# A decode attention kernel: the last group's output sum moves from two halves of 288 columns to four quarters of 144, stored as 8 rows

## Chip, cores and metric

The kernel runs on one core of one Trainium2 chip. The metric is the device time of one execution in microseconds (us). The core has five engines with a queue each: TensorE (PE; its weight loads are listed apart as PEld), VectorE (DVE), ScalarE (ACT), GpSimd (POOL) and SyncE (SP), which here only issues DMA transfers. Matmuls write into PSUM, where a bank holds 512 float32 columns in each of 128 partitions; everything else lies in SBUF.

## What is computed

Two independent problems, A and B, each one decode step of attention over the last 4096 positions of a key and value cache, with 2 batch rows, 32 query heads that share 16 key/value heads in pairs, and 128 elements a head. The two outputs of 576 columns are put side by side.

```python
def _A_ref(x, k_cache, v_cache, wq, wo):          # _B_ref is the same
    B, Sq, D = x.shape                            # 2, 1, 576
    Hq, Dh = 32, 128
    Hkv, Sk = k_cache.shape[1], k_cache.shape[2]  # 16, 16384
    W = min(4096, max(256, Sk // 4))
    rep = Hq // Hkv
    q = (x @ wq).reshape(B, Sq, Hq, Dh).transpose(0, 2, 1, 3)
    k = jnp.repeat(k_cache[:, :, Sk - W:, :], rep, axis=1)
    v = jnp.repeat(v_cache[:, :, Sk - W:, :], rep, axis=1)
    scores = jnp.einsum("bhqd,bhkd->bhqk", q, k) * (Dh ** -0.5)
    p = _softmax(scores, axis=-1)
    o = jnp.einsum("bhqk,bhkd->bhqd", p, v)
    return o.transpose(0, 2, 1, 3).reshape(B, Sq, Hq * Dh) @ wo
...
return jnp.concatenate([a, b], axis=-1)
```

Everything is bfloat16 in memory. Reading the caches, wq and wo moves 153 MB.

## The kernel before

The program is written out by hand: `S.add` appends an operation to one engine's queue with a list of the operations that it depends on, and the loops from line 834 to line 923 fix the order on every queue. Waits on semaphores are derived from the dependencies when the queues are emitted (line 976). A DMA is an operation of SP (`dma_op`) with a semaphore of its own kind.

**Stages.** The two problems' 16 key/value heads are handled in 16 steps `s` (8 for A, 8 for B), each of which covers 4 pairs of batch row and key/value head. A step loads a 4 MB slab of K and one of V into a ring of four (`issue_slab`, line 239). DVE transposes the K slab in four pieces (`do_X`, L515), PE multiplies with the queries into the PSUM tile `ST[s % 2]` (`do_S`, L540 and, through the helper `matmul_again`, L188), ACT takes the exponential (L585), DVE transposes the result, and PE multiplies with V into `ACC` (`do_PV`, L631). That last product uses four column groups of the array: `ACC[32*cb:32*cb+32]`, cb from 0 to 3, all in one bank.

**Groups.** Two steps make a group G (0 to 7; 0 to 3 are problem A). A group's attention outputs are normalised (`do_norm`) into `oTg`, spread over a mask (`om`), redistributed on PE (`do_redist`, L739) and copied by ACT into `Rsb` (L757): one column per batch row and head slot, so that a head's two batch rows are a weight matrix of 128 x 2. `do_proj` (line 766) multiplies with that head's 128 rows of wo. For groups 0 to 6 (`by_group`) the 576 output columns go to `OT` (512, L786) and to a bank of the pair `TB` (the other 64, through L188), and the 64 columns are summed in `o_rest` (L802, L805).

**The last group.** For group 7 the wo rows come last of all, in four DMAs: `wo3` (line 291) for its first step, and `issue_last` (line 277), three transfers `wl0` (heads 0 and 1), `wl1` (head 2), `wl2` (head 3) for its second. Ahead of them, once group 6 is done, the sum so far is moved into the PSUM tile `ST[0]`, which is free by then. `fin(half)` names where (line 763): half 0 is partitions 0 and 1 of the first bank, half 1 partitions 32 and 33 of the second bank, 288 columns each. The move is `fin0` on ACT (L810), `fin1` on DVE (L811, the 64 columns of `o_rest` and `TB`) and `fin2` on DVE (L813, 224 columns). All three are in the list `fin_ops`, of which the last is waited for by three idle matmuls on PE (line 749) and by the first step's projection. The projection of the last group is line 790: each of 4 + 4 heads is two matmuls of 288 columns, in two column groups. The weights of the first four heads are `Rsb[1][:, :, s]`, of the last four `oTn[:, h, :]`, which `do_norm` writes directly (L719).

**The end.** `do_E(1)` casts the two halves to bfloat16 into `out_sb[1]`, which is the tile `pR`: ACT takes half 0 (L822), DVE half 1 (L823). `do_out` (line 830) stores 2 rows of 576 elements, 1152 bytes each, with one DMA; SP waits for it at the end (line 985). Problem A's output is stored by the same function from `out_A`, whose issue stands just ahead of it in SP's queue. The other masks are slices of the tile `masks` (lines 156 and 157).

Of the kernel before, what the change touches and what calls it, by code (L numbers as in the profile page):

```python
# [5 lines left out]
FP32 = mybir.dt.float32  # L6
# [53 lines left out]
def build_kernel(nc, probs, out, cfg=None):  # L60
# [30 lines left out]
    NOUT = wo0.shape[1]  # L91
    NH = NOUT // 2
    NB0 = 512
    NB1 = NOUT - NB0
    assert NOUT % 2 == 0 and 0 < NB1 <= NB0
    SCALE = float(Dh) ** -0.5
# [10 lines left out]
    def by_group(G):  # L107
        return G < NG - 1
# [5 lines left out]
    with es:  # L114
# [36 lines left out]
        maskB = sb("maskB", [128, 512], BF16)  # L151
        oTn = sb("oTn", [128, 4, Bb], BF16)
        oTg = [sb("oTg%d" % n_, [128, n], BF16) for n_, n in enumerate((64, 32))]
        om = sb("om", [128, 2, 256], BF16)
        Rsb = [sb("Rsb%d" % n_, [128, Bb, n], BF16) for n_, n in enumerate((32, 16))]
        masks = sb("masks", [128, 30], BF16)
        maskS, mask16D, maskA, mask4S, maskJ, maskP = (masks[:, a_:b_] for a_, b_ in ((0, 8), (8, 16), (16, 20), (20, 24), (24, 28), (28, 30)))
        mask16S = sb("mask16S", [128, 16], BF16)
# [5 lines left out]
        acc_r = sb("acc_r", [128, 2, 128], BF16)  # L164
        o_rest = sb("o_rest", [Bb, NB1], FP32)
        ident_r = sb("ident_r", [128, 32], BF16)
        out_A = sb("out_A", [Bb, NOUT], BF16)
        out_sb = [out_A[:, :], pR[0:Bb, 0:NOUT]]
        ps = lambda name, shape: es.enter_context(nc.psum_tensor(name, shape, FP32))
# [514 lines left out]
        def do_norm(D_):  # L684
# [5 lines left out]
            if by_group(G):  # L690
# [23 lines left out]
                return  # L714
            dst = oTn[:, :, :].rearrange("d (t r) b -> d b t r", t=2) if sl else \
                oTg[u % 2][:, 0:8].rearrange("d (b r t) -> d b t r", b=Bb, r=2)
# [14 lines left out]
        def do_redist(u, idle=0):  # L731
# [22 lines left out]
            if u >= 2:  # L754
                g2, n2 = UNITS[u - 2]
                deps.append(proj[2 * (g2 + n2 - 1) + 1])
            r_ev[u] = S.add("act", lambda e: e.activation(  # L757
                Rsb[u % 2][:, :, 0:NS], bank[:, 0:NS * Bb].rearrange("d (b s) -> d b s", b=Bb), ACTF.Copy), deps, "rev%d" % u)
            tb_consumer[n] = r_ev[u]

        fin_ops = []

        def fin(half):
            return ST[(ND - 2) % 2][32 * half:32 * half + Bb, 512 * half:512 * half + NH]

        def do_proj(D_):
# [4 lines left out]
            w0 = wo_slot(G)  # L771
            new = G % GPP == 0
            if by_group(G):
                parts = [([(Rsb[u % 2][:, :, s0 + s_], s_) for s_ in range(8)], [r_ev[u], wo_dma[G]], new, True, True)]
            elif D_ < ND - 1:
                parts = [([(Rsb[u % 2][:, :, s_], s_) for s_ in range(4)], [r_ev[u], wo_dma[G]] + fin_ops, False, False, False)]
            else:
                parts = [([(oTn[:, h, :], 4 + h) for h in hs], [norm[D_], wo_last[n_]], False, False, n_ == len(HEADS) - 1)
                         for n_, hs in enumerate(HEADS)]
            for lhs, deps, start, rstart, rstop in parts:  # L780
                def f(e, rest, lhs=lhs, start=start, rstart=rstart, rstop=rstop):
                    last = None
                    for n_, (l_, s_) in enumerate(lhs):
                        begin, end = n_ == 0, n_ == len(lhs) - 1
                        if by_group(G):
                            first = e.matmul(OT[0:Bb, 0:NB0], l_, wob[:, w0 + s_, 0:NB0], start=start and begin, stop=end, skip_group_check=True)  # L786
                            last = matmul_again(e, first, rest[0:Bb, 0:NB1], wob[:, w0 + s_, NB0:NOUT], rstart and begin, rstop and end)
                        else:
                            for half in range(2):
                                last = e.matmul(fin(half), l_, wob[:, w0 + s_, half * NH:(half + 1) * NH],  # L790
                                                start=False, stop=end, skip_group_check=True)
                    return last
                deps = deps + [e_ops[(P - 1, 0)]]
                if by_group(G):
                    n, bank, proj[D_] = tb_job(f, "proj%d" % D_, deps)
                    rest_at[G] = bank
                    if G % GPP < GPP - 1 and G < NG - 2:
                        d = [proj[D_]]
                        if new:
                            if P:  # L800
                                d.append(e_ops[(P - 1, 1)])
                            rest_add[G] = S.add("dve", lambda e: e.tensor_copy(o_rest[:, :], bank[0:Bb, 0:NB1]), d, "rest%d" % G)  # L802
                        else:
                            d.append(rest_add[G - 1])
                            rest_add[G] = S.add("dve", lambda e: e.tensor_tensor(o_rest[:, :], o_rest[:, :], bank[0:Bb, 0:NB1], ALU.add),  # L805
                                                d, "rest%d" % G)
                        tb_consumer[n] = rest_add[G]
                    elif G == NG - 2:
                        d = [proj[D_], chain[(ND - 2, "exp")], chain[(ND - 2, "max")]]
                        a_ = S.add("act", lambda e: e.activation(fin(0), OT[0:Bb, 0:NH], ACTF.Copy), d, "fin0")  # L810
                        tb_consumer[n] = S.add("dve", lambda e: e.tensor_tensor(  # L811
                            fin(1)[:, NB0 - NH:NH], o_rest[:, :], bank[0:Bb, 0:NB1], ALU.add), d + [rest_add[G - 1]], "fin1")
                        fin_ops.append(S.add("dve", lambda e: e.tensor_copy(fin(1)[:, 0:NB0 - NH], OT[0:Bb, NH:NB0]), [a_], "fin2"))  # L813
                    else:
                        rest_at[G] = (n, bank)
# [3 lines left out]
        def do_E(P):  # L819
            G = (P + 1) * GPP - 1  # L820
            if G == NG - 1:
                e_ops[(P, 0)] = S.add("act", lambda e: e.activation(out_sb[P][:, 0:NH], fin(0), ACTF.Copy), [proj[2 * G + 1]], "Elo%d" % P)  # L822
                e_ops[(P, 1)] = S.add("dve", lambda e: e.tensor_copy(out_sb[P][:, NH:NOUT], fin(1)), [proj[2 * G + 1]], "Ehi%d" % P)  # L823
                return
            n, bank = rest_at[G]
            e_ops[(P, 1)] = tb_consumer[n] = S.add("dve", lambda e: e.tensor_tensor(
                out_sb[P][:, NB0:NOUT], o_rest[:, :], bank[0:Bb, 0:NB1], ALU.add), [proj[2 * G + 1], rest_add[G - 1]], "Ehi%d" % P)
            e_ops[(P, 0)] = S.add("act", lambda e: e.activation(out_sb[P][:, 0:NB0], OT[0:Bb, 0:NB0], ACTF.Copy), [proj[2 * G + 1]], "Elo%d" % P)

        def do_out(P, c0, c1, eng, deps):  # L830
            dma_op(eng, out_sem, 1, lambda e: e.dma_start(
                out[:, 0, P * NOUT + c0:P * NOUT + c1], out_sb[P][:, c0:c1]).then_inc(out_sem, 16), deps, "out%d_%d" % (P, c0))

# [88 lines left out]
        for P in range(NPROB):  # L922
            do_out(P, 0, NOUT, "sp", [e_ops[(P, 1)], e_ops[(P, 0)]])

# [99 lines left out]
```

## Time and profile before

| | |
|---|---|
| median of 3 runs | 362.61 us (362.55 to 362.83) |
| the execution with the profile | 363.02 us |
| its span, first to last instruction | 361.8 us |
| mean granted TensorE clock | 0.882 of full speed |
| loads | 153.10 MB, 423 GB/s over the span |
| DVE transposes of K, L515 | 145.3 us busy in 64 instructions |
| matmuls with the queries, L540 and L188 | 111.6 and 110.1 us |
| cast of half 0, L822, ACT, 2x288 | 400 ns |
| cast of half 1, L823, DVE, 2x288 | 449 ns |
| move of the sum: L810, L811, L813 | 361, 222, 393 ns |
| issue of the last store, L831 | 263 ns |

The profile gives each engine's busy time, the span in 40 equal slices (digits are tenths), the waits between engines and the chain that ended last, which is followed back from the last instruction through whatever released each step. In a line of the timeline stand start and length in us, engine, line of the code, operation, what is written and read, and the shape; "128*2" is the part of the PE array that is used, "x4" a count, and the bracket the idle time before it with what ended it. "SPq" is SP's queue of DMA issues. Times of instructions are of the profiled execution.

### The profile page before, as it was taken

How to read it: one execution, taken by the hardware profiler on the slowest of the kernel's cores; microseconds unless marked ns; L12 is line 12 of the kernel's file. 1: busy time of each engine (PE TensorE's matmuls, PEld its weight loads, DVE VectorE, ACT ScalarE, POOL GpSimd, SP SyncE). 2: the span in 40 equal slices, each digit the busy share in tenths (PEclk: the TensorE clock that was granted, in tenths of full speed). 3: DMA queues.
4: the chain of work that ended last, by engine and by line, in shares of the span. 5: the costliest groups of instructions: out<-in, count | busy, mean ns of one | idle time of the engine just before them, and what ended most of it. 6: DMA issues, size and time to landing. Idle time of an engine off the chain costs nothing.

```text
span 361.8 us, 2730 instructions
## 1 busy us (share of the span) xinstructions
PE 218.6 (60%) x1318; PEld 55.8 (15%) x945; DVE 200.9 (56%) x175; ACT 68.2 (19%) x149; POOL 35.3 (10%) x55
## 2 busy tenths in 40 slices
PE   0399195763747207466574737766867707657786
PEld 0010021120111101112120201212121201211132
DVE  4112599846647019283756658392919239079931
ACT  1036502130203002103020203020201203002131
POOL 1000000004000400001300040002100040200020
PEclk9999689997889857969698978899898978969999
DMA  8999999999999999999999999999999999999996
GB/s 348 421 449 406 464 406 437 431 408 453 415 442 438 428 424 438 429 428 438 417 446 422 435 428 442 426 435 428 424 424 440 431 424 433 431 438 428 438 409 248
DMA packets 6491, 153.27 MB, mean 424 GB/s; under 512 B 712, under 2 KB 1232, under 8 KB 1616
## 3 DMA queue, kind: packets, MB, share of 16 engines
q1 hardware_dynamic: 6476, 153.10, 98.8%
q8 instruction: 9, 0.15, 0.2%
q14 instruction: 2, 0.02, 0.0%
q10 hardware_dynamic: 4, 0.00, 0.0%
HBM read 153.10 MB, written 0.00 MB: 423 GB/s over the span
## 4 chain that ended last, share of the span: by engine, by line
DMA 72%; DVE 17%; PE 7%; ACT 3%; SPq 1%; issue 0%
DMA ring<-in_B_k_cache_dram 34%; DMA ring<-in_A_k_cache_dram 27%; DVE xt L515 14%; DMA wob<-in_B_wo_dram 8%; DMA wob<-in_B_x_dram 3%; PE st L188 3%; PE st L540 3%; ACT wob L465 1%; DVE wob L475 1%; ACT qk L483 1%; PE st L450 1%; DVE m L550 1%; ACT wob L470 1%; DVE nM L563 0%; SPq L252 0%
## 5 line engine op out<-in xcount | busy, mean ns | idle before, releaser
L515 DVE STREAM_TRANSPOSE xt<-ring 128x2048 f32<-128x2048 f32 x64 | 145.3, 2284 | 86.6 <-DMA ring<-in_A_k_cache_dram 49.8
L540 PE MATMUL st<-xt,zq 128*128 128x512 bf16 x256 | 111.6, 436 | 122.6 <-DVE xt L515 98.1
L188 PE MATMUL st<-xt,zq 128*128 128x512 bf16 x256 | 110.1, 430 | 0.0
L540 PEld LDWEIGHTS st<-xt,zq 128*128 128x128 bf16 x256 | 27.1, 106 | 216.3 <-DVE xt L515 113.5
L631 PE MATMUL acc<-ring,pC 128*32 128x512 bf16 x512 | 32.5, 381 | 1.2 <-DMA ring<-in_B_v_cache_dram 1.2
L568 ACT ACTIVATE nMrep<-nM 1x128 f32<-1x128 f32 x16 | 4.9, 308 | 146.9 <-DVE nM L563 146.9
L643 ACT ACTIVATE acc_sb<-acc 128x512 bf16<-128x512 f32 x16 | 9.5, 596 | 79.9 <-PE acc L631 79.9
L593 DVE STREAM_TRANSPOSE pC<-pR 128x1024 bf16<-128x1024 bf16 x16 | 19.6, 1223 | 3.7 <-ACT pR L585 2.1
L650 POOL TENSOR_TENSOR acc_sb<-acc_sb,masks 128x1024 bf16<-128x1024 bf16 (+1 forms) x8 | 13.4, 1679 | 66.6 <-ACT acc_sb L643 66.6
L550 DVE TENSOR_REDUCE m<-st 128x1 f32<-128x1024 f32 x16 | 19.0, 1190 | 1.4 <-PE st L188 1.4
L502 POOL TENSOR_TENSOR zq<-qk,masks 128x128 bf16<-128x128 bf16 x16 | 6.3, 398 | 136.2 <-PE st L188 114.4
L585 ACT ACTIVATE pR<-st,bias_sb 128x1024 bf16<-128x1024 f32 x16 | 17.8, 1114 | 0.5
L475 DVE STREAM_TRANSPOSE wob<-wob 128x512 f32<-128x512 f32 x8 | 5.7, 711 | 20.3 <-ACT wob L465 12.9
L415 ACT ACTIVATE st<-maskB 128x1024 f32<-128x1024 bf16 x16 | 16.5, 1032 | 1.6 <-POOL rsel L600 0.4
L786 PE MATMUL ot<-wob,Rsb 128*2 128x512 bf16 x56 | 15.2, 390 | 0.0
L631 PEld LDWEIGHTS acc<-ring,pC 128*32 128x32 bf16 x512 | 12.4, 96 | 15.9 <-issue 3.2
L600 POOL TENSOR_TENSOR rsel<-masks,rsum 128x16 f32<-128x16 bf16 x8 | 1.7, 216 | 108.0 <-ACT pR L585 108.0
L188 PE MATMUL tb<-wob,Rsb 128*2 128x64 bf16 x56 | 10.9, 195 | 0.0
L375 PE MATMUL tb<-wob 4*128 4x16 bf16 x5 | 0.3, 179 | 14.5 <-DVE wob L380 14.5
L653 POOL TENSOR_TENSOR acc_sb<-acc_sb 128x512 bf16<-128x512 bf16 (+1 forms) x8 | 8.2, 1029 | 0.6
L188 PE MATMUL st<-ring,wob 128*128 128x512 bf16 x24 | 7.9, 445 | 0.0
L579 ACT ACTIVATE bias_sb<-tb 128x1 f32<-128x1 f32 x16 | 2.7, 171 | 24.8 <-PE tb L573 24.8
(89 smaller groups left out, 99.5 us busy)
## 6 DMA issues: line engine op xcount, KB each, us to landing
ring<-in_A_k_cache_dram SPq DMA_DIRECT2D x8, 4096.0 KB, 30.4
ring<-in_A_v_cache_dram SPq DMA_DIRECT2D x8, 4096.0 KB, 32.5
ring<-in_B_k_cache_dram SPq DMA_DIRECT2D x8, 4096.0 KB, 28.4
ring<-in_B_v_cache_dram SPq DMA_DIRECT2D x7, 4096.0 KB, 32.8
wob<-in_A_wo_dram SPq DMA_DIRECT2D x1, 4608.0 KB, 43.3
ring<-in_A_wq_dram SPq DMA_DIRECT2D x1, 4096.0 KB, 12.7
ring<-in_B_wq_dram SPq DMA_DIRECT2D x1, 4096.0 KB, 22.6
ring<-in_B_v_cache_dram SPq DMA_DIRECT2D x1, 3072.0 KB, 25.5
```

Of the source, the lines that this page charges most:

```text
L188: return e.add_instruction(mybir.InstMatmult(name=nc.get_next_instruction_name(), engine=i.engine, ins=[e.lower_ap(rhs), i.ins[1]], outs=[ ...
L415: chain[(s, "fill")] = S.add("act", lambda e: e.activation(ST[s % 2][:, :].rearrange("k (h j) -> k h j", h=2), maskB[:].unsqueeze(1).broad ...
L475: chain[(G, "qtr")] = S.add("dve", lambda e: e.transpose(qtr[:].bitcast(FP32), qrow[:].bitcast(FP32)), evs, "qtr%d" % G)
L515: Xop[(s, u)] = S.add("dve", lambda e: e.transpose(xt[:, i % NKT, :].rearrange("k (j w) -> k j w", w=64), ring[:, n % NR, :].bitcast(FP32) ...
L540: first = last = e.matmul(bank, zq[:, p4, s % NZQ, w0:w0 + 128], mv, start=False, stop=stop, skip_group_check=True)
L550: chain[(s, "max")] = S.add("dve", lambda e: e.tensor_reduce(m1[:, 0:1], ST[s % 2][:, :], AX.X, ALU.max), d, "max%d" % s)
L585: chain[(s, "exp")] = S.add("act", lambda e: e.activation(pR[:, :], ST[s % 2][:, :], ACTF.Exp, bias=bias_sb[:, 0:1], scale=SCALE, accum_ou ...
L593: chain[(s, "pC")] = S.add("dve", lambda e: e.transpose(pC[:, s % NPT, :, :].rearrange("k j c -> k (j c)"), pR[:, :]), d, "pC%d" % s)
L631: last = e.matmul(ACC[32 * cb:32 * cb + 32, 0:512], pC[:, D_ % NPT, j0_:j0_ + 4, :].rearrange("k j c -> k (j c)"), ring[:, n % NR, j0_ * 1 ...
L643: acc_ev[D_] = S.add("act", lambda e: e.activation(acc_sb[:, D_ % 2, :], ACC[:, :], ACTF.Copy), d, "accev%d" % D_)
L650: t = S.add("pool", lambda e: e.tensor_tensor(v, v, maskJ[:].unsqueeze(1).unsqueeze(3).broadcast_to([128, l1 - l0, 4, 128]), ALU.mult), [a ...
L786: first = e.matmul(OT[0:Bb, 0:NB0], l_, wob[:, w0 + s_, 0:NB0], start=start and begin, stop=end, skip_group_check=True)
```

## The change

The last group's sum is kept in one bank of `ST[0]`: quarter q, 144 columns, at the partitions from 32q on. In each quarter batch row 0 is at partition 32q and batch row 1 at 32q + 16, so a weight matrix spans 17 columns, of which the first and the last are meant; what the 15 between them add goes to partitions that nobody reads. To have that spacing without copies, problem B's head columns in `Rsb` and those in `oTn` are laid out 16 apart, and the weights are a run of 17 neighbouring columns; the free columns of `oTn` hold four of the masks. Problem B's earlier groups (4 to 6) use the same 17 columns, so `OT`, the bank of `TB` and `o_rest` have 17 rows there. Problem A keeps its two rows.

Each head of the last group is four matmuls of 144 columns instead of two of 288. The move of the sum is three ACT copies of 144 columns, a DVE add of 64 and a DVE copy of 80. Each final cast takes two quarters at once: ACT partitions 0 to 48, DVE 64 to 112, 144 columns. The store takes every 16th partition: 8 rows of 144 elements (288 bytes), written as quarter, batch row, column.

```diff
-        oTn = sb("oTn", [128, 4, Bb], BF16)
+        oTn = sb("oTn", [128, Bb * BS], BF16)                 # BS = 16
...
-        Rsb = [sb("Rsb%d" % n_, [128, Bb, n], BF16) for n_, n in enumerate((32, 16))]
+        Rsb = [sb("Rsb%d" % n_, [128, Bb * n], BF16) for n_, n in enumerate((32, BS))]
+        def of_slot(u, s_):
+            return by_row(u)[:, :, s_] if u == 0 else Rsb[u % 2][:, s_:s_ + RB]   # RB = 17
...
-        out_sb = [out_A[:, :], pR[0:Bb, 0:NOUT]]
+        out_q = pR[:, 0:NQ]                                    # NQ = 144
...
-        def fin(half):
-            return ST[(ND - 2) % 2][32 * half:32 * half + Bb, 512 * half:512 * half + NH]
+        fin_all = ST[(ND - 2) % 2]
+        def fin(q):
+            return fin_all[32 * q:32 * q + RB, 0:NQ]
...
-                parts = [([(oTn[:, h, :], 4 + h) for h in hs], ...
+                parts = [([(oTn[:, h:h + RB], 4 + h) for h in hs], ...
...
-                            for half in range(2):
-                                last = e.matmul(fin(half), l_, wob[:, w0 + s_, half * NH:(half + 1) * NH],
+                            for q in range(4):
+                                last = e.matmul(fin(q), l_, wob[:, w0 + s_, q * NQ:(q + 1) * NQ],
                                                 start=False, stop=end, skip_group_check=True)
...
-                        a_ = S.add("act", lambda e: e.activation(fin(0), OT[0:Bb, 0:NH], ACTF.Copy), d, "fin0")
+                        def f_fin(e):
+                            last = None
+                            for q in range(3):
+                                last = e.activation(fin(q), OT[0:RB, q * NQ:(q + 1) * NQ], ACTF.Copy)
+                            return last
+                        a_ = S.add("act", f_fin, d, "fin0")
...
-                            fin(1)[:, NB0 - NH:NH], o_rest[:, :], bank[0:Bb, 0:NB1], ALU.add), ..., "fin1")
-                        fin_ops.append(S.add("dve", lambda e: e.tensor_copy(fin(1)[:, 0:NB0 - NH], OT[0:Bb, NH:NB0]), [a_], "fin2"))
+                            fin(3)[:, NB0 - 3 * NQ:NQ], o_rest[:, :], bank[0:RB, 0:NB1], ALU.add), ..., "fin3")
+                        fin_ops.append(S.add("dve", lambda e: e.tensor_copy(fin(3)[:, 0:NB0 - 3 * NQ], OT[0:RB, 3 * NQ:NB0]), [a_], "fin4"))
...
-                e_ops[(P, 0)] = S.add("act", lambda e: e.activation(out_sb[P][:, 0:NH], fin(0), ACTF.Copy), ..., "Elo%d" % P)
-                e_ops[(P, 1)] = S.add("dve", lambda e: e.tensor_copy(out_sb[P][:, NH:NOUT], fin(1)), ..., "Ehi%d" % P)
+                e_ops[(P, 0)] = S.add("act", lambda e: e.activation(out_q[0:32 + RB, :], fin_all[0:32 + RB, 0:NQ], ACTF.Copy), ..., "Elo%d" % P)
+                e_ops[(P, 1)] = S.add("dve", lambda e: e.tensor_copy(out_q[64:96 + RB, :], fin_all[64:96 + RB, 0:NQ]), ..., "Ehi%d" % P)
...
-        def do_out(P, c0, c1, eng, deps):
-            dma_op(eng, out_sem, 1, lambda e: e.dma_start(
-                out[:, 0, P * NOUT + c0:P * NOUT + c1], out_sb[P][:, c0:c1]).then_inc(out_sem, 16), deps, "out%d_%d" % (P, c0))
+        def do_out(P):
+            to = out[:, 0, P * NOUT:(P + 1) * NOUT]
+            to, src = (to, out_A[:, :]) if P < NPROB - 1 else (to.rearrange("b (q c) -> q b c", q=4), out_q[0:128:BS, :])
+            dma_op("sp", out_sem, 1, lambda e: e.dma_start(to, src).then_inc(out_sem, 16), [e_ops[(P, 1)], e_ops[(P, 0)]], "out%d" % P)
```

## The prediction

> **What bounds the kernel now.** I read first the page's busy shares and slices, then the chain that ended last, then the last three microseconds in order of time. The slices say that the 16 DMA engines are full from the second slice to the last but one, while no compute engine is over 60%:
>
> ```profile
> PE 218.6 (60%) x1318; PEld 55.8 (15%) x945; DVE 200.9 (56%) x175; ACT 68.2 (19%) x149; POOL 35.3 (10%) x55
> DMA  8999999999999999999999999999999999999996
> ```
>
> So 153 MB of loads set nearly the whole span, and a change behind them can only move what comes after the last load. The end of the chain of waits shows that part (start, length, what; times in us):
>
> ```profile
> 331.87 27.84 DMA wob<-in_B_wo_dram
> 359.71 0.04 issue
> 359.75 0.31 PE st L790 x2
> 360.06 0.02 issue
> 360.08 0.45 DVE pR L823
> ```
>
> The last 128 rows of wo land at 359.71; two matmuls of 288 columns, a cast, and then the store. The same stretch in order of time, with shapes:
>
> ```profile
> 359.07 0.12 PEld L790 LDWEIGHTS st<-wob,oTn 128*2 128x2 bf16 x4 [0.29 <-DVE oTn L719]
> ...
> 359.40 0.08 PEld L790 LDWEIGHTS st<-wob,oTn 128*2 128x2 bf16 x2 [0.22 <-DMA wob<-in_B_wo_dram]
> 359.75 0.08 PEld L790 LDWEIGHTS st<-wob,oTn 128*2 128x2 bf16 x2 [0.27 <-DMA wob<-in_B_wo_dram]
> 360.08 0.40 ACT L822 ACTIVATE pR<-st 2x288 bf16<-2x288 f32 x1 [1.88 <-PE st L790]
> 360.08 0.45 DVE L823 CAST pR<-st 2x288 bf16<-2x288 f32 x1 [1.37 <-PE st L790]
> 360.57 0.26 SPq L831 DMA_DIRECT2D out_dram<-pR  x1
> ```
>
> Heads 0 and 1, head 2 and head 3 each start when their load lands, 0.33 us apart, so PE waits for the DMA. The store's issue ends at 360.83, and SP's last wait shows what is left:
>
> ```profile
> SPq L985 <- DMA out_dram<-pR: 0.9, 1, 0.9
> ```
>
> From landing to end: 0.04 + 0.31 + 0.02 + 0.45 + 0.04 + 0.26 + 0.9 = 2.0 us, up to 361.7 of a span of 361.8. The execution with the profile took 363.02 us (1.2 around the span), 0.41 above the median 362.61 of the runs; I carry the change found in the span over to the median.
>
> **Part 1, matmuls of the last group.** Each head goes from two of 288 columns to four of 144, each with its own weight load of 17 columns instead of 2, in four column groups of one bank. A record of 288 columns lasts 283 ns, one of 512 (L631, same full clock) 378 ns: 0.42 ns a column, so 144 last 222 ns, 61 less. Do four run side by side? Line 631 has this form, four column groups in one bank:
>
> ```profile
> 344.85 1.05 PE L631 MATMUL acc<-ring,pC 128*32 128x512 bf16 x16
> ...
> 358.26 0.26 PE L678 MATMUL tb<-ident_r,acc_sb 128*128 128x8 bf16 x4
> ```
>
> Four rounds of four take 1.05 us; less the last one's 0.38 that is 0.22 a round, the price of one 512-column stream: they run together, and the records of a round start within 10 ns. So the last head ends 61 - 6 = 0.055 us sooner. The other bound is L678, where four pairs on the whole array start 0.03 us apart ((0.26 - 0.17) / 3): the last pair would start 0.09 late and end 0.09 + 0.22 - 0.29 = 0.02 later than now. Loads of 17 columns lie between those of 2 (78 ns) and 32 (96 ns), so up to 0.015 more. I take -0.055, since L631 has the same form; bounds -0.06 to +0.04. The extra pairs ahead (16 of line 790 for slot 0, 8 for heads 0 and 1) have 0.63 us from 358.44 to 359.07 and 0.33 us to head 2; at the worst price, 0.03, they need 0.48 and 0.24, so waiting for the weights hides them. Without it they would cost 0.1.
>
> **Part 2, casts.** 2x288 becomes 49x144 on ACT and DVE. ACT: rows of 128x512 (594 ns) and 128x8 (172) give 0.84 ns a column, and 172 + 280 x 0.84 = 407 against the 400 measured on two partitions, so rows cost nothing; 144 columns last 400 - 121 = 279. DVE: the cast of 288 lasts 449, the add of 64 (L811) 222, so 1.01 a column and 303 ns; from L813 (224 columns, 393 ns) the slope is 0.88 and it is 323. DVE still ends last: -0.13 to -0.146, I take -0.14. Both casts now read one bank at the same time, which no row of before shows (they read two). Bounds: 0, or one behind the other, +0.28. I take 0, because the two touch different partitions, as the four matmuls of L631 do.
>
> **Part 3, the store.** Two rows of 1152 bytes become eight of 288, from partitions 16 apart, with a two-dimensional pattern on the DRAM side. Issue: the 2-row form took 263 and 313 ns on SP, the slab loads with two dimensions on one side and 128 rows 534 to 621 (median 535). The new one has few rows and two dimensions: between 0 and +0.27; as few rows as the first, the pattern of the second, I take about a third, +0.10. Packets: the trace has two data packets of 48 ns starting 40 ns apart (361.315 and 361.355) on two DMA engines, each with a semaphore packet of 9 ns behind. If eight rows use four engines, the last starts 0.08 later and its two short packets need about as long as one of 48 ns (4 bytes take 9, so 288 take some 19 by the line between). One engine for all: 8 x 19 = 0.15, 0.10 more than now. Eight engines: 6 x 0.04 = +0.24. I take +0.07, bounds 0 to +0.24. The Trainium skill, page DMA: Bandwidth & Descriptors, section "Why a DMA increments its semaphore by 16 and not by 1", says a transfer uses the largest number of engines up to 16 that divides both sides' outer sizes. The two packets of before agree with it; here, 8 and 4 would give four engines, the same +0.08.
>
> **Part 4, what is hidden.** Moving the sum into the bank: one ACT copy of 2x288 (361 ns) becomes three of 144 (361 - 121 = 240 each, 0.72), then a DVE copy of 80 instead of 224 columns (393 - 144 x 1.01 = 0.25 instead of 0.39). It ends at 354.25 + 0.72 + 0.02 + 0.25 = 355.24 instead of 355.04; the first that waits for it is PE's idle matmul at 357.48, and ACT's and DVE's next works are at 357.54 and 358.55, so 2.2 us of cover; without it +0.2. Problem B's earlier projections get 17 weight columns for 2, hidden since each pair streams 576 columns (0.245 us). The masks only change address. 32 more PE instructions pull an instruction fetch forward that now starts at 358.81, 16 KB on one DMA engine over 1.04 us:
>
> ```profile
> q8 instruction: 1, 0.02, 2.5%
> ```
>
> Up to 0.2 us earlier, at half rate, it can delay that engine's last weights by 0.1; I take 0, since this holds for one engine in 16 being also the last.
>
> **Sum**: -0.055 - 0.14 + 0.10 + 0.07 = -0.03 us: 362.61 - 0.03 = 362.58, put as 362.6. A measurement of this kernel can tell about 0.2%, 0.73 us, from no change; everything that the change shortens, 0.31 + 0.45, is hardly more than that.
>
> **Rivals.**
> (a) The store costs what it did: -0.055 - 0.14 = -0.20, 362.4. For it: few bytes. Against it: eight rows, two dimensions. Not distinguishable from no change.
> (b) A hidden cover fails inside the tail: casts in turn (+0.28) or matmuls in turn with a later fetch (+0.075 + 0.1): 362.7 to 362.9. For it: neither is in the trace. Against it: L631's four groups.
> (c) The other side, slower: the short rows are written in two passes. If the memory must fetch what a 288-byte row does not fill before it writes, the store's wait after issue, 0.9 us, is paid up to once more: 362.58 + 0.9 = 363.5; twice, for two rows in turn on one engine, 364.4. It decides from 0.76 us on. For it: rows of 288 bytes that neighbours on other engines share blocks with; before has no write under 1152 bytes. Against it: semaphores of loads land about 0.38 us after their packet and the store's 0.34, so no receipt from DRAM shows. The Trainium skill, same page, section "Specifications", says that below 512 bytes a DMA engine reads, modifies and writes; no run here shows it yet.
> (d) Faster by over 0.73: matmuls, casts and more would have to vanish, or the stream of loads run 0.2% quicker, which the change does not touch. Nothing in the profile speaks for it but the scatter between executions (363.02 against 362.61).
>
> **How the numbers follow.** Forecast 0.45, (a) 0.2, (b) 0.1, (c) 0.17, (d) 0.08. Faster by over 0.2%: 0.08 (d). Slower: (c), 0.17. Within: 0.75. The range: low is (a)'s 362.4 less 0.2 for casts and packets at their better ends and the runs' scatter; high is 363.6, which takes in the upper bounds of the unknowns (0.04 + 0.27 + 0.24 - 0.13 = +0.42, with casts in turn +0.70) and (c)'s single pass.
>
> **What would show it.** In the changed trace: four matmuls of 144 columns starting within some 10 ns after the last weights, casts of about 0.28 and 0.30 us that start together, an issue of 0.3 to 0.45, eight packets of 288 bytes on four engines, and SP's last wait at 0.9 to 1.0. Pairs 0.03 apart or casts in turn show (b). A last wait of 1.6 us or more shows (c) and makes the forecast wrong; so does a last load of wo that lands at another time after the stream by over half a microsecond.

## The result, and the profile after

| | before | changed |
|---|---|---|
| median of 22 runs each | 362.85 us | 363.23 us |
| ratio, 95% interval | | 1.0014 (1.0008 to 1.0020) |
| execution with the profile | 363.02 | 363.19 |
| last weights landed, in its span | 359.71 | 359.37 |
| from that landing to the end of SP's last wait | 2.03 | 2.46 |

The changed kernel is slower by 0.14%, about 0.5 us by the ratio and 0.38 by the medians. The time lies in the range and within 0.2%, but the direction is clear of the scatter and is not the -0.03 us of the sum. The last landing itself moves between executions, from 359.37 to 359.99 in the runs below, so a few tenths of a microsecond are best read in the tail, as the distance from that landing to the end: 0.43 us longer.

The end of the chain of waits, changed kernel (start, length, what):

```profile
331.52 27.85 DMA wob<-in_B_wo_dram
359.37 0.04 issue
359.42 0.27 PE st L806 x4
359.68 0.02 issue
359.71 0.31 DVE pR L844
```

The same stretch in order of time, changed kernel:

```profile
359.41 0.10 PEld L806 LDWEIGHTS st<-wob,oTn 128*17 128x17 bf16 x4 [0.26 <-DMA wob<-in_B_wo_dram]
359.71 0.28 ACT L843 ACTIVATE pR<-st 49x144 bf16<-49x144 f32 x1 [1.84 <-PE st L806]
359.71 0.31 DVE L844 CAST pR<-st 49x144 bf16<-49x144 f32 x1 [1.33 <-PE st L806]
360.08 0.67 SPq L854 DMA_DIRECT2D out_dram<-pR  x1
```

The matmuls take 0.27 us for 0.31, the casts 0.28 and 0.31 for 0.40 and 0.45: what the change meant to shorten is shorter. The store's issue is 0.67 us for 0.26. SP's own waits, changed kernel (waited for what, us in total, times, longest):

```profile
SPq L1007 <- DMA out_dram<-pR: 1.1, 1, 1.1
```

The wait behind the issue is also longer, 1.1 for 0.9. The packets from the issue of the last store to its end, with the rate in 40 equal slices of that stretch, first the kernel before (1.18 us):

```profile
GB/s 0 0 0 0 0 0 0 0 0 0 0 0 0 0 0 0 0 0 0 0 0 0 0 0 0 39 39 0 0 0 0 0 0 0 0 0 0 0 0 0
DMA packets 4, 0.00 MB, mean 2 GB/s; under 512 B 2, under 2 KB 4, under 8 KB 4
```

and the changed kernel (1.75 us):

```profile
GB/s 0 0 0 0 0 0 0 0 0 0 0 0 0 0 0 0 0 0 0 0 0 0 0 0 0 0 0 0 0 0 40 13 0 0 0 0 0 0 0 0
DMA packets 12, 0.00 MB, mean 1 GB/s; under 512 B 12, under 2 KB 12, under 8 KB 12
```

Two rows and two semaphore packets became eight and four; with one semaphore packet an engine, as the prediction counts, the store uses four DMA engines where it used two. In the packet records of the trace the first one starts 1.316 us after the issue's start instead of 0.744; all twelve then start within 0.08 us, as the four before did. The time is lost before the first byte moves.

### The profile page after: what moved, and what is told of

Its sections match the earlier page's. It is cut to its first block, busy times and chain, and to the rows that moved or that the text cites. A ratio compares the mean times of both kernels' runs of the same rounds, so it can differ in the third digit from the quotient of the medians.

```text
span 361.9 us, 2762 instructions
## 1 busy us (share of the span) xinstructions
PE 221.7 (61%) x1332; PEld 56.6 (16%) x961; DVE 200.6 (55%) x175; ACT 68.7 (19%) x151; POOL 35.3 (10%) x55
## 4 chain that ended last, share of the span: by engine, by line
DMA 71%; DVE 17%; PE 7%; ACT 3%; SPq 1%; issue 0%
DMA ring<-in_B_k_cache_dram 33%; DMA ring<-in_A_k_cache_dram 27%; DVE xt L528 14%; DMA wob<-in_B_wo_dram 8%; DMA wob<-in_B_x_dram 3%; PE st L201 3%; PE st L553 3%; ACT wob L478 1%; DVE wob L488 1%; ACT qk L496 1%; PE st L463 1%; DVE m L563 1%; ACT wob L483 1%; DVE nM L576 0%; SPq L265 0%
## 5 line engine op out<-in xcount | busy, mean ns | idle before, releaser
L553 PE MATMUL st<-xt,zq 128*128 128x512 bf16 x256 | 113.9, 445 | 118.4 <-DVE xt L528 92.9
L201 PE MATMUL st<-xt,zq 128*128 128x512 bf16 x256 | 112.3, 439 | 0.0
L644 PE MATMUL acc<-ring,pC 128*32 128x512 bf16 x512 | 33.3, 388 | 1.7 <-DMA ring<-in_B_v_cache_dram 1.7
L663 POOL TENSOR_TENSOR acc_sb<-acc_sb,oTn 128x1024 bf16<-128x1024 bf16 (+1 forms) x8 | 13.4, 1679 | 68.9 <-ACT acc_sb L656 68.9
L802 PE MATMUL ot<-wob,Rsb 128*2 128x512 bf16 (+1 forms) x56 | 14.7, 380 | 0.0
L613 POOL TENSOR_TENSOR rsel<-oTn,rsum 128x16 f32<-128x16 bf16 x8 | 1.7, 218 | 108.9 <-ACT pR L598 108.9
L201 PE MATMUL tb<-wob,Rsb 128*2 128x64 bf16 (+1 forms) x56 | 10.8, 193 | 0.0
```

What stands on the lines that cost most here:

```text
L201: return e.add_instruction(mybir.InstMatmult(name=nc.get_next_instruction_name(), engine=i.engine, ins=[e.lower_ap(rhs), i.ins[1]], outs=[ ...
L553: first = last = e.matmul(bank, zq[:, p4, s % NZQ, w0:w0 + 128], mv, start=False, stop=stop, skip_group_check=True)
L644: last = e.matmul(ACC[32 * cb:32 * cb + 32, 0:512], pC[:, D_ % NPT, j0_:j0_ + 4, :].rearrange("k j c -> k (j c)"), ring[:, n % NR, j0_ * 1 ...
L663: t = S.add("pool", lambda e: e.tensor_tensor(v, v, maskJ[:].unsqueeze(1).unsqueeze(3).broadcast_to([128, l1 - l0, 4, 128]), ALU.mult), [a ...
L802: first = e.matmul(OT[0:nr, 0:NB0], l_, wob[:, w0 + s_, 0:NB0], start=start and begin, stop=end, skip_group_check=True)
```

## The experiments

All times "to the end" count from the landing of the last wo rows; "issue" is the length of SP's DMA instruction, "first packet" is counted from its start. An issue of 0.24 to 0.33 us is called cheap here, one of 0.55 us or more dear. Where no ratio is given, the kernel was run once, with the profile.

### The store put back, and the store alone

```diff
-            to, src = (to, out_A[:, :]) if P < NPROB - 1 else (to.rearrange("b (q c) -> q b c", q=4), out_q[0:128:BS, :])
+            to, src = (to, out_A[:, :]) if P < NPROB - 1 else (to, pR[0:Bb, 0:NOUT])
```

> The changed kernel with the last store put back to its old form: 2 rows of 576 elements (1152 bytes) out of partitions 0 and 1 of the same tile, so problem B's output is not the product's. Theory S (the whole loss is the store): the matmuls and casts keep what they gained in the changed kernel, so the time from the landing of the last wo rows to the end falls from 2.46 us to 2.03 - 0.05 - 0.14 = 1.84 us, the issue is back at 0.26 us, and the kernel is 0.2 us faster than before (ratio about 0.9995). Theory R (the loss is elsewhere: 17 weight columns, 32 more PE instructions, an earlier instruction fetch that delays the last weights): the ratio stays near 1.0014 less the few hundredths of the store, that is over 1.0005.

Measured: ratio 0.9999 (0.9990 to 1.0008); issue 0.263, first packet 0.745, 1.88 us to the end. In order of time, this kernel:

```profile
360.32 0.28 ACT L843 ACTIVATE pR<-st 49x144 bf16<-49x144 f32 x1 [1.81 <-PE st L806]
360.32 0.31 DVE L844 CAST pR<-st 49x144 bf16<-49x144 f32 x1 [1.30 <-PE st L806]
360.70 0.26 SPq L854 DMA_DIRECT2D out_dram<-pR  x1
```

Short casts and a cheap issue stand together here, and the tail is 0.15 us shorter than before's 2.03. The interval of the ratio is too wide to tell the 0.9995 expected from 1, so this gain is read from one trace.

The other way round, in the kernel before:

```diff
         def do_out(P, c0, c1, eng, deps):
+            if P:
+                to = out[:, 0, P * NOUT:(P + 1) * NOUT].rearrange("b (q c) -> q b c", q=4)
+                dma_op(eng, out_sem, 1, lambda e: e.dma_start(to, pR[0:128:16, 0:NOUT // 4]).then_inc(out_sem, 16), deps, "out1")
+                return
```

> The kernel before with the last store alone changed: 8 rows of 144 elements from every 16th partition of the tile, written as quarter, batch row, column, as in the changed kernel; the casts and matmuls are the old ones, so what is stored for problem B is not the product's output. Theory S: issue 0.67 us instead of 0.26, first data packet 1.3 us after the issue's start instead of 0.74, the kernel is 0.6 us slower than before (ratio about 1.0017). Theory R: ratio within 0.0005 of 1.

Measured: ratio 1.0015 (1.0006 to 1.0024); issue 0.674, first packet 1.309, 2.61 us to the end. In order of time, the kernel before with the new store:

```profile
359.90 0.40 ACT L822 ACTIVATE pR<-st 2x288 bf16<-2x288 f32 x1 [1.86 <-PE st L790]
359.90 0.45 DVE L823 CAST pR<-st 2x288 bf16<-2x288 f32 x1 [1.35 <-PE st L790]
360.39 0.67 SPq L833 DMA_DIRECT2D out_dram<-pR  x1
```

The store alone adds 2.61 - 2.03 = 0.58 us; the rest of the change alone takes 0.15 off. Together 0.43, which is what the changed kernel lost. That the loss is the store is shown from both sides.

### Which property of the store

Each of four runs replaces the same line of the changed kernel, here in short form:

```diff
-... (to.rearrange("b (q c) -> q b c", q=4), out_q[0:128:BS, :])
+... (out[0, 0, :].rearrange("(r c) -> r c", r=8), out_q[0:128:BS, :])        # q_rows8_1d, A's store left out
+... (to.rearrange("b (q c) -> b q c", q=4), pR[0:Bb, 0:640] as b, 4 pieces 160 apart, 144 of each)   # q_rows2_2d
+... (to, pR[0:32:16, 0:NOUT])                                               # q_two16
+... (to.rearrange("b (q c) -> q b c", q=4), out_q[0:8, :])                  # q_adj8
```

> The changed kernel with 8 rows of 144 elements written one behind the other (one dimension of rows on the DRAM side) over the first batch row's 1152 columns; problem A's store is left out and the output is not the product's. Theory D (the second dimension on the DRAM side costs): the issue falls to 0.3 us or less and the first packet comes 0.8 us after the issue's start. Theory N (eight short rows cost, whatever the pattern): the issue stays at 0.6 us or over and the first packet at 1.2 us or over.

> The changed kernel with a store from partitions 0 and 1 alone, each giving four pieces of 144 elements that stand 160 apart, so that there are two dimensions and 8 pieces of 288 bytes but 2 partitions; problem B's output is not the product's. Theory D (dimensions): issue 0.6 us or over. Theory N (pieces of 288 bytes, eight of them): issue 0.6 us or over too, so it is told from D by the run with 8 rows in one dimension. Theory P (the partitions, 8 of them 16 apart, cost): issue about 0.26 us.

> The changed kernel with a store of 2 rows of 576 elements from partitions 0 and 16; problem B's output is not the product's. Theory T (step): issue 0.6 us or over. Theory C (count): 0.26 us, as from partitions 0 and 1.

> The changed kernel with a store of 8 rows of 144 elements from the neighbouring partitions 0 to 7, written as quarter, batch row, column; problem B's output is not the product's. Theory T (step): issue 0.26 to 0.3 us, first packet at 0.8 us. Theory C (count): 0.67 us and 1.3 us, as from every 16th partition.

| store | issue | first packet | to the end |
|---|---|---|---|
| 8 rows 16 apart, one dimension (q_rows8_1d) | 0.690 | 1.33 | 2.48 |
| 2 partitions, 4 pieces each (q_rows2_2d) | 0.277 | 0.76 | 1.92 |
| partitions 0 and 16 (q_two16) | 0.721 | 1.36 | 2.48 |
| 8 neighbouring partitions as 4 x 2 (q_adj8) | 0.774 | 1.41 | 2.56 |

SP's issue in the four traces, in the order of the table:

```profile
360.25 0.69 SPq L855 DMA_DIRECT2D out_dram<-pR  x1
360.11 0.28 SPq L854 DMA_DIRECT2D out_dram<-pR  x1
360.23 0.72 SPq L854 DMA_DIRECT2D out_dram<-pR  x1
360.09 0.77 SPq L854 DMA_DIRECT2D out_dram<-pR  x1
```

Theory D, which my forecast had leant on, falls: one dimension is as dear as two, and two dimensions with eight pieces of 288 bytes are cheap. N falls with the second row of the table. Two partitions 16 apart are dear, so it isn't the count (C); eight neighbouring ones are dear too, so it isn't the step alone (T). No single property named so far fits all four.

### One store per batch row

```diff
...
+            for b, eng in enumerate(("sp", "act")):          # q_batch_sp: ("sp", "sp")
+                to = out[b, 0, P * NOUT:(P + 1) * NOUT].rearrange("(q c) -> q c", q=4)
+                src = out_q[BS * b:128:2 * BS, :]
+                dma_op(eng, out_sem, 1, lambda e, to=to, src=src: e.dma_start(to, src).then_inc(out_sem, 16), deps, ...)
```

> The changed kernel with the last store split by batch row, and the product's output: 4 partitions 32 apart into 576 neighbouring columns, one issued by SP, one by ScalarE's queue behind its cast. Theory C (the issue's time goes with the number of partitions beyond two): 4 partitions take about 0.4 us each, at once on two queues, so from the last landing to the end 2.46 - 0.27 = 2.2 us and the time is 0.2 us under the changed kernel, ratio about 1.0005. Theory T (it is the step between the partitions): each issue 0.67 us as now, 2.4 us or more, ratio about 1.0014. If 4 partitions are as cheap as 2: 1.9 us, ratio about 0.9996.

> The same two stores by batch row, both issued by SP one behind the other. Theory C: 0.4 us each, the second's first packet 0.45 us after the first's, so 2.5 us from the last landing to the end. Theory T: 0.67 us each, about 3.1 us. If 4 partitions are as cheap as 2: 0.26 us each and 2.2 us.

Measured on two queues: issues of 0.606 and 0.639, 2.73 us to the end, ratio 1.0021 (1.0012 to 1.0030). On SP alone: 0.639 and 0.554, 3.01 us. Four partitions 32 apart are as dear as eight 16 apart, and two queues at once are worse than one store: their first packets start 1.26 us (ScalarE's queue) and 1.6 us (SP's) after the issues, not together.

### Is it the first store of its form?

In the kernel before, problem A's store has the same form as the last one and stands ahead of it. So the changed kernel got a forerunner, an earlier store of the new form, and from the kernel before A's store was taken away.

```diff
...
+            warm = dma_op("sp", out_sem, 1, lambda e: e.dma_start(to, maskB[0:128:BS, 0:NQ]).then_inc(out_sem, 16), [init["maskB"]], "warm")
+            dma_op("sp", out_sem, 1, lambda e: e.dma_start(to, out_q[0:128:BS, :]).then_inc(out_sem, 16), [warm] + deps, "out%d" % P)
```

> The changed kernel with one DMA more in SP's queue: right behind problem A's store, 28 us before the end, a store of the last one's own form (8 rows of 144 elements from every 16th partition, two dimensions on the DRAM side) writes rows of a constant tile where the last store will write; the last store then overwrites them, so the output is the product's. Theory F (the first store of a form on SP's queue pays 0.4 us, a repeated one does not; the two-row store was cheap because problem A's store of the same form stands ahead of it): the last issue falls from 0.67 to 0.3 us, its first packet from 1.32 to about 0.8 us after the issue's start, from the last landing to the end 1.95 us instead of 2.46, and the kernel is slightly faster than the one before, ratio about 0.9998. Theory I (the price lies in the form itself, each time: neighbouring partitions 0 and 1 are cheap, any other set is dear): issue 0.67 again, ratio 1.0014.

```diff
-        for P in range(NPROB):
+        for P in range(1, NPROB):
             do_out(P, 0, NOUT, "sp", [e_ops[(P, 1)], e_ops[(P, 0)]])
```

> The kernel before without problem A's store (its half of the output stays unwritten), so that the last store is the first one of its kind since the load of x at the start. Theory F: the issue of the last store rises from 0.26 to 0.6 us or over, and its first packet from 0.74 to 1.2 us or over. Theory I: 0.26 and 0.74, as before.

With the forerunner: issue 0.582, first packet 1.22, 2.39 us to the end, ratio 1.0012 (1.0003 to 1.0021). Without A's store: 0.275 and 0.75, 2.04. Theory F falls; the forerunner saves 0.09 of the 0.41, no more. The forerunner's own issue, behind the queued loads of wo, took 7.25 us (L858), and A's two-row store at that place 1.05 us in the kernel before and 1.13 in the changed one. So the prices of the forms here are those of a queue with no loads in flight.

### The forms by themselves

Stores behind the last one, each issued when the one ahead had landed, every form twice.

```diff
...
+        def probe(fn):
+            for _ in range(2):
+                probes.append(dma_op("sp", out_sem, 1, lambda e: fn(e).then_inc(out_sem, 16), [probes[-1] if probes else S.ops["sp"][-1]], "probe"))
...
+        probe(lambda e: e.dma_start(halves, wide[0:2, :]))                    # L934: partitions 0, 1
+        probe(lambda e: e.dma_start(row(2, 576), wide[0:2, :]))               # L935
+        probe(lambda e: e.dma_start(halves, wide[0:4:2, :]))                  # L936: 0, 2
+        probe(lambda e: e.dma_start(halves, wide[0:32:16, :]))                # L937: 0, 16
+        probe(lambda e: e.dma_start(halves, wide[32:34, :]))                  # L938: 32, 33
...
+        probe(lambda e: e.dma_start(row(8, 144), wide[0:8, 0:144]))           # L941: 0 to 7
+        probe(lambda e: e.dma_start(row(8, 144), wide[0:128:16, 0:144]))      # L942: every 16th
+        probe(lambda e: e.dma_start(quarters, wide[0:128:16, 0:144]))         # L943: the changed form
...
```

> The kernel before, with 24 more stores behind the last one, each issued by SP when the one ahead has landed: twelve forms, each twice, out of a tile of weights into the output, which is no longer the product's. They measure the issue, and issue to landing, by form alone, with no other transfer in flight. In order: partitions 0 and 1 (old form), the same into neighbouring rows, partitions 0 and 2, 0 and 16, 32 and 33, then 4, 3 and 8 neighbouring partitions, 8 of every 16th, the same as quarter by batch row (changed form), 16 neighbouring ones of 64 elements, one partition. Theory P (two neighbouring partitions are the cheap form, any other set is dear): 0.26 us for partitions 0 and 1 and 32 and 33, 0.55 us or more for the others, the second of a pair up to 0.1 less than the first. Theory A (partition 0 as the start with few rows is cheap, the address and not the set counts): 32 and 33 dear, 0 and 2 cheap. Theory N (the number of rows counts): 0 and 2 and 0 and 16 cheap here, and 3, 4, 8, 16 rising in order.

The DMA instructions by line, first set of probes (durations in ns, least, median, most; then when they started):

```profile
L934 SPq DMA_DIRECT2D out_dram<-wob x2: 235/236/236, 361.8 to 363.0; - x2
L936 SPq DMA_DIRECT2D out_dram<-wob x2: 621/682/743, 366.4 to 368.2; - x2
L937 SPq DMA_DIRECT2D out_dram<-wob x2: 563/564/564, 369.9 to 371.5; - x2
L938 SPq DMA_DIRECT2D out_dram<-wob x2: 240/241/242, 373.1 to 374.3; - x2
L941 SPq DMA_DIRECT2D out_dram<-wob x2: 276/276/277, 379.9 to 381.1; - x2
L942 SPq DMA_DIRECT2D out_dram<-wob x2: 592/602/613, 382.3 to 384.0; - x2
L943 SPq DMA_DIRECT2D out_dram<-wob x2: 547/556/565, 385.6 to 387.3; - x2
```

Neighbouring partitions are cheap from partition 0 and from partition 32 (L934, L938), and in every number tried: 2, 3, 4, 8 and 16 took 0.24, 0.24, 0.25, 0.28 and 0.33 us. A step of 2 is already as dear as one of 16 (L936, L937). From issue to the last landing it is 1.12 us for two neighbouring rows of 1152 bytes, 1.17 for eight of 288, and 1.62 to 1.68 for eight with a step. All three theories of the expectation fall: every run of neighbours tried is cheap. What remained was q_adj8, eight neighbours at 0.774 us. The second set kept the partitions and changed how the memory side is split:

```diff
...
+        probe(lambda e: e.dma_start(row(8, 144), wide[0:8, 0:144]))           # L936: 8 rows
+        probe(lambda e: e.dma_start(quarters, wide[0:8, 0:144]))              # L937: 4 x 2
+        probe(lambda e: e.dma_start(pairs, wide[0:4, 0:288]))                 # L938: 2 x 2
+        probe(lambda e: e.dma_start(pieces4, wide[0:8, 0:144]))               # L939: 2 x 4
+        probe(lambda e: e.dma_start(halves.rearrange("b (q c) -> b q c", q=2), wob[0:2, 0:2, 0:288]))   # L940: 2 x 2, both sides
+        probe(lambda e: e.dma_start(row(8, 144), wide[0:16:2, 0:144]))        # L941: step 2
+        probe(lambda e: e.dma_start(quarters, wide[0:128:16, 0:144]))         # L942: the changed form
```

> The kernel before with 14 more stores behind the last one, each issued when the one ahead has landed, seven forms twice each; the output is not the product's. In order: 8 neighbouring partitions into 8 rows one behind the other; the same partitions written as quarter by batch row (4 x 2); 4 neighbouring partitions written as half by batch row (2 x 2); 8 neighbouring partitions written as batch row by quarter (2 x 4, a merged run on the memory side in each batch row); 2 neighbouring partitions with two pieces each on both sides (2 x 2); 8 partitions, every second, into 8 rows; the changed store. Theory E (either costs: a step between the partitions, or memory rows split otherwise than the partitions): 0.28, then 0.55 to 0.77 for the second, third and fourth, 0.27 for the fifth, 0.6 for the sixth and 0.56 for the last; a store that has both costs no more than one that has one. Theory M (the step alone costs; the 0.77 was something else in that run): the second, third and fourth at 0.3 or less.

The same view, second set:

```profile
L936 SPq DMA_DIRECT2D out_dram<-wob x2: 275/276/276, 361.7 to 362.9; - x2
L937 SPq DMA_DIRECT2D out_dram<-wob x2: 664/722/780, 364.1 to 365.9; - x2
L938 SPq DMA_DIRECT2D out_dram<-wob x2: 614/618/621, 367.7 to 369.4; - x2
L939 SPq DMA_DIRECT2D out_dram<-wob x2: 605/610/615, 371.1 to 372.8; - x2
L940 SPq DMA_DIRECT2D out_dram<-wob x2: 254/257/260, 374.4 to 375.6; - x2
L941 SPq DMA_DIRECT2D out_dram<-wob x2: 647/676/704, 376.8 to 378.5; - x2
L942 SPq DMA_DIRECT2D out_dram<-wob x2: 567/574/580, 380.3 to 381.9; - x2
```

Theory E holds in all seven: a store is dear when its partitions are not neighbours, or when the memory side splits the rows otherwise than the partitions do (L937 to L939), and one that has both costs no more than one that has one (L942). Two dimensions that match on both sides are cheap (L940). In the three dear splits the two sides also differ in the number of dimensions; no run has two unequal splits with the same number.

The probes also say more on the forerunner: the saving does not need the same form. The changed form took 0.674 us in the changed kernel, where the store ahead was a cheap one, and 0.582 behind the forerunner of its own form; behind dear stores of another form it took 0.55 to 0.58 (L943 in the first set, L942 in the second).

### Versions that keep the short casts

```diff
+            return fin_all[32 * q:32 * q + Bb, 0:NQ]                          # q_pairs: rows 32q, 32q + 1
...
+        for q in range(4):
+            dma_op("act" if q < 2 else "sp", out_sem, 1, lambda e, q=q: e.dma_start(
+                out[:, 0, NOUT + q * NQ:NOUT + (q + 1) * NQ], pR[32 * q:32 * q + Bb, 0:NQ]).then_inc(out_sem, 16),
+                [e_ops[(1, q // 2)]], "out1_%d" % q)
```

> A version meant to keep the shorter casts and use only cheap stores, with the product's output: the quarters in one bank as in the changed kernel, but batch rows on neighbouring partitions (2 weight columns, rows 32q and 32q + 1), casts of 34 x 144, and four stores of 2 neighbouring rows x 144, two issued by ScalarE's queue as soon as its own cast is done, two by SP behind VectorE's. From the last landing to the end: 0.04 + 0.27 + 0.02 + 0.31 + 0.04 + 0.24 + 0.04 for the first issue, then 1.13 for the second, 2.09 us against 2.03 before and 2.46 changed: ratio about 1.0002, so no gain over the kernel before but 0.4 us under the changed one. If the two queues get in each other's way, as when both issued at once before (ScalarE's stores 0.3 us behind): 2.4 us, ratio 1.001.

Measured: ratio 1.0008 (0.9999 to 1.0017); all four issues cheap (0.257, 0.268 on ScalarE's queue, 0.263, 0.329 on SP's), 2.30 us to the end. The tail is 0.42 us longer than the 1.88 of q_store2, which has short casts and one cheap store. Four cheap stores, two on each queue, so cost more than the 0.15 that casts and matmuls save, and 0.2 more than expected.

```diff
+            g_ = (0, 2, 1, 3)[q]                                              # q_shift
+            return fin_all[32 * g_:32 * g_ + Bb, 0:NQ]
...
+                e_ops[(P, 1)] = S.add("dve", lambda e: e.tensor_copy(pR[0:32 + Bb, NQ:2 * NQ], fin_all[64:96 + Bb, 0:NQ]), ...)
...
+        for h, eng in enumerate(("act", "sp")):
+            dma_op(eng, out_sem, 1, lambda e, h=h: e.dma_start(
+                out[:, 0, NOUT + 2 * h * NQ:NOUT + 2 * (h + 1) * NQ], pR[32 * h:32 * h + Bb, 0:2 * NQ]).then_inc(out_sem, 16), ...)
```

> A version with the short casts, cheap stores and the product's output: batch rows on neighbouring partitions, the four column groups hold quarters 0, 2, 1, 3, ScalarE casts groups 0 and 1 into columns 0 to 143 of the store's tile and VectorE casts groups 2 and 3 into columns 144 to 287 of the same 34 partitions, so that partitions 0 and 1 hold columns 0 to 287 of the output and partitions 32 and 33 the rest; two stores of 2 neighbouring rows x 288, one by ScalarE's queue and one by SP, at once. From the last landing to the end 0.04 + 0.27 + 0.02 + 0.31 + 0.04 + 1.17 + 0.1 for two queues at once = 1.95 us against 2.03 before and 2.46 changed; ratio to before 0.9998, to the changed kernel 0.9986. If the casts' lower length does not carry over, or the two queues cost more than 0.2 us, 2.05 us or more and no gain.

Measured: ratio 1.0000 (0.9991 to 1.0010), 2.01 us to the end. In order of time, this kernel:

```profile
360.09 0.28 ACT L830 ACTIVATE pR<-st 34x144 bf16<-34x144 f32 x1 [1.83 <-PE st L793]
360.09 0.31 DVE L831 CAST pR<-st 34x144 bf16<-34x144 f32 x1 [1.32 <-PE st L793]
360.46 0.26 ACTq L932 DMA_DIRECT2D out_dram<-pR  x1
360.46 0.26 SPq L932 DMA_DIRECT2D out_dram<-pR  x1
```

Both stores are cheap and start together, but the later one's completion lands 1.30 us after the issue's start where a lone store's landed after 1.15. So 0.45 of the changed kernel's tail comes back in the profile, and the tail is level with the kernel before. No version was found that beats it.

## Why the prediction was wrong, point by point

**What bounds the kernel**: right. The loads fill the span, and the whole difference lies behind the last landing.

**Part 1, matmuls**: right. The four records of the last head start within 10 ns of each other (359.415 to 359.425) and last 230 ns; from the landing to the casts it is 0.335 us for 0.372, -0.04 where -0.055 was forecast. The rest is in the records: 230 ns for the forecast 222, and the last of four starts 10 ns behind the first where the last of two started 5. Weights of 17 columns cost about 0.006 us: with 2 columns (q_pairs, q_shift) the same records last 224 ns, and from the landing to the casts it is 0.328 and 0.330. The other new pairs, ahead of the last head, cost nothing that shows: the heads still wait for their loads.

**Part 2, casts**: the lengths are right (0.284 and 0.310 against 0.279 and 0.303), so reading one bank at once cost 5 and 7 ns over these estimates at the most. The gain on the path is 0.115, not 0.14, because the path runs over the other engine: in every tail in which SP waits for the two casts and nothing else, its issue starts 0.09 us after the end of ACT's cast, whose signal it waits for first, and VectorE's, later by 0.03 to 0.05, has come by then. ACT's cast fell by 0.116.

**Part 3, the store, is the step that failed.** The sum had +0.10 for the issue and +0.07 for the packets; measured are +0.41 for the issue, 0.674 against 0.263, and +0.16 between its end and the first packet, 0.642 against 0.481, for which the sum had no term; spread over four engines, the packets add 0.01. So +0.58 stood where +0.17 was put: -0.04 - 0.115 + 0.58 = +0.43. The mechanism that I priced, few rows and a second dimension, isn't the one: q_rows2_2d has both and is as cheap as the old form. The slab loads, from which the upper bound of +0.27 came, do have one of the two properties that decide for the store: in `issue_slab` their memory side is 32 x 4 rows, against 128 neighbouring partitions. The forecast took a third of that bound because the store has few rows, but eight rows cost no less than 128 (0.674 against 0.535), and the store went 0.14 over the bound itself. No DMA of before is a short store with either property, so a load was no bound on it. Eight rows on four engines, by the Trainium skill (DMA: Bandwidth & Descriptors, "Why a DMA increments its semaphore by 16 and not by 1"), is what came: four semaphore packets, and eight where eight rows stood on both sides (q_rows8_1d).

**Part 4, what is hidden**: right. The move of the sum ended at 354.73, the idle matmuls started at 357.14 (only its last part, `fin2`, renamed `fin4`, is in `fin_ops`; the parts ahead come before it on VectorE or are what it waits for). The instruction fetch started at 358.71 instead of 358.81, and the loads still landed in their order.

**Rivals.** (a) and (b) fell: the store changed, and neither casts nor matmuls went in turn. (c) had the side right and the cause wrong: rows of 288 bytes from neighbouring partitions land 1.17 us after the issue, eight of them, against 1.12 for two of 1152 (probes), so no second pass is seen. The Trainium skill's sentence on transfers under 512 bytes (same page, "Specifications") may hold, but no time for it shows in this store. The 0.76 us that (c) needed was not reached. (d) did not happen.

**The range** held the measured 363.23, but not for the reasons that set it. Of the 0.65 between 362.58 and 363.23, 0.24 is the base: the median of before is 362.85 over 22 runs, and was 362.61 over three. And the sum of the unknowns at their upper ends, +0.42, comes close to the +0.43 measured by luck: matmuls at +0.04 and packets on eight engines at +0.24 did not come, an issue beyond its upper end and a later first packet did. The prediction also took 0.73 us as the least that can be told from no change; with 22 runs each the interval is 0.06% to either side, some 0.2 us, so the loss of about 0.4 stands clear.

What stays open is what the sequencer does in those 0.4 us, why the first packet then comes 0.16 later, and why a dear store behind another dear one saves up to 0.1; the runs show when it happens, not how.

## What to carry to other kernels

At the end of a kernel a short store is paid in full, so its form is part of the critical path: take rows from neighbouring partitions, and split the memory side as the partitions are split (shown here for 1 to 16 partitions). A layout that makes the compute ahead of it faster can cost more in the store than it gains (here 0.15 us against 0.58); measure a new DMA form by itself, in a few probe stores at the end of the kernel, before the layout is built around it. And where two engines feed one wait, read which signal the waiting queue takes first.

## What the hardware showed that I had not expected

- With no loads in flight, the issue of a small store by SP took 0.24 to 0.33 us for 1 to 16 neighbouring partitions. It took 0.55 to 0.78 for 2, 4 or 8 partitions 2, 16 or 32 apart, and for 4 or 8 neighbours whose rows the memory side splits otherwise. The first packet followed about 0.48 us after the end of the issue in the first case, about 0.64 in the second.
- Behind the queued loads of wo the same issues are longer: 0.64 to 1.38 us for A's two-row store in the traces that have it (1.05 in the kernel before), 7.25 for the eight-row form in its one run (q_warm).
- ScalarE's queue pays the same: 0.606 for four rows 32 apart, 0.26 for two neighbours.
- Of two cheap stores issued at the same moment on two queues, the later lands 0.15 us later than one alone would; two dear ones' first packets start some 0.35 us apart.
- Two engines reading different partitions of one bank at the same time took 284 and 310 ns, against 279 and 303 estimated from the slopes of their longer instructions.
